# Retention and a mixture of experts in one kernel: moving work and tests at the seams between stages

## The chip, the cores and the metric

The kernel runs on one core of one Trainium2 chip. The metric is the device time of one execution in microseconds. A core has five engines that run side by side and wait for each other by semaphores: TensorE (PE in the profile; PEld is its loading of the stationary operand), VectorE (DVE), ScalarE (ACT), GpSimd (POOL) and SyncE (SP). Copies between memory and the core are started by an engine's queue and carried out by DMA engines.

## The reference, cut to what matters

Two blocks follow each other. The first is a retention layer: for each of 4 batches and 8 heads a 64x64 state decays and takes up one outer product per time step, over 768 steps. Its output, 3072 rows (tokens) of 512, goes to a mixture of experts: each token goes to the one expert out of 8 with the largest logit, whose two layers are 512 to 1024 and 1024 to 512.

```
state = gamma * state + k[t] v[t]^T          # per batch and head
y[t]  = q[t] @ state / sqrt(64)
x = y, heads side by side: (3072, 512)
logits = x @ w_gate;  e = argmax(logits);  gate = softmax(logits)[e]
out = gate * (max(x @ w1[e], 0) @ w2[e])     # no token is dropped, however many an expert gets
```

## The kernel before

The retention is computed in 24 steps of 128 time steps, ordered so that the four batches of one chunk make a group; there are 6 groups. A step loads q, k and v (`load`), scales and transposes them (`scale_and_transpose`), and does the masked products and the state (`retain`).

After each group, `place` finds each of its 512 tokens' expert, gate and rank within the expert, and stores the gated rows x to memory. It is written as a generator: each `yield` ends a piece, and the main loop takes a few pieces after each step, so that they lie between the matmuls of later steps.

```python
def place(c):                       # cut
    ... parts = wg^T x  (4 matmuls of 512 columns), lgT = copy          # L314, L317
    yield
    ... lg (logits), max, exp, one-hot oh, gate                         # L321 to L340
    yield
    rk = ... ; rank, col, prow, at, val, here                           # L343 to L373
    yield
    found = sum over b of here[b]^T val[b];  inv += found               # L377, L380
    yield
    x = xg[c % 2]
    for b in range(B):
        tr = ps("tr", 3, "trx")...
        for dt in range(DT):
            nc.tensor.transpose(tr[:, dt, :], xT[:, dt, b, :], ident)   # L388
        nc.scalar.activation(out=x[:, b, :]..., in_=tr, func=AF.Copy, scale=gate[:, b : b + 1])
        if b == 1:
            yield
    nc.scalar.dma_start(x_d[ts(c, B * P), :]..., x)                     # L393
    if c == NC - 2:
        ... tot, pad: at least 256 tokens of expert 0
        early.append(index(inv[:, :, 0 : EARLY // P], "_e"))
        gather(xs2[0], early[0][0], range(EARLY // P), (c + 1) * B * P)  # L160
```

The main loop and the **fixed job**: the first 256 tokens of expert 0 are known after five groups, so their two layers are computed while the sixth group is placed.

```python
for n in range(len(steps)):
    if n + AHEAD < len(steps): load(n + AHEAD)
    if n == 17: wa = weights(first, 0)
    if n + 1 < len(steps): scale_and_transpose(n + 1)
    retain(n)
    for _ in range(2 if n < len(steps) - B else 3): next(rest, None)
    if steps[n][1] == B - 1: rest = place(steps[n][0])

with tc.manual_schedule(engines={PE}):
    turn(xs2[0], xTa, range(EARLY // P), nc.vector.tensor_copy)     # transposes of gathered rows, L190
    for f in range(FT):
        layer1(EARLY, xTa, wa[0], hTa, f)                           # L198, ScalarE relu L200
        if f != 4: next(rest, None)
    for _ in rest: pass
    for t in range(EARLY // P):
        layer2(EARLY, hTa, wa[1], oa, t)                            # L210, ScalarE copy L213
scatter(oa, early[0][1], range(EARLY // P))                         # L217
```

Then the tokens per expert are counted, and for each expert an **arm** is chosen: the same job compiled for a number of rows, in steps of 32 up to 512. Engines load the arm's number into a register and branch. `switch_hint` tells an engine ahead of time where it will branch to.

```python
cnt = ...; nc.tensor.matmul(cnt, lhsT=ones_b, rhs=acc[:, NC, :], ...)   # L446
ne, arm = ...                        # VectorE, L449 to L457
src_i, dst_i = index(inv, "")        # rows to gather and to scatter, for all experts
...
sets = [wa, weights(keep2, 1)]       # keep2 takes memory that the fixed job's tiles held
with tc.manual_schedule(engines={PE, ACT, POOL}):
    gather(xs2[1], cols[0][0], range(HALF, TC))      # the rest of expert 0
    gather(xs2[0], cols[1][0], range(TC))            # expert 1
    which = regs(0)                                  # value_load of arm, L481
    tc.switch_hint(which, arms_of(0), label="job0")
    xT = mp.tile(...)
    turn(xs2[1], xT, range(HALF, TC), nc.vector.tensor_copy)
    for e in range(E):
        nxt = regs(e + 1)                            # not for the last
        for a in tc.Switch(which, arms_of(e), hint=f"job{e}"):
            n = STEP * (LEAST + a)
            ... 8 x layer1; turn of the next expert's rows; layer2 per 128 rows; the last job scatters in its arm
        scatter(...); gather(... e + 2); weights(... e + 2)

more = nc.values_load(over[0:1, 0:1], min_val=0, max_val=1)             # L520, on every engine
with tc.If(more > 0), ...:                                              # L521
    ... further jobs for experts with more than 512 tokens; with the given inputs not taken
```

Of the kernel before, what the change touches and what calls it, by code (L numbers as in the profile page):

```python
# [54 lines left out]
def kernel(  # L55
# [47 lines left out]
    nc.sync.dma_start(dec, decay)  # L103
# [119 lines left out]


    with ExitStack() as actx:
# [80 lines left out]
        def place(c):  # L306
# [34 lines left out]
            yield  # L341
            rk = ps("tr", 3, "rk")[:, 0 : B * E].rearrange("p (b e) -> p b e", e=E)
# [38 lines left out]

            yield

            x = xg[c % 2]
            for b in range(B):
                tr = ps("tr", 3, "trx").rearrange("p (a t) -> p a t", a=DT)
                for dt in range(DT):
                    nc.tensor.transpose(tr[:, dt, :], xT[:, dt, b, :], ident)  # L388
                nc.scalar.activation(out=x[:, b, :].rearrange("p (a t) -> p a t", a=DT), in_=tr, func=AF.Copy,
                                     scale=gate[:, b : b + 1])  # L390
                if b == 1:
                    yield
            nc.scalar.dma_start(x_d[ts(c, B * P), :].rearrange("(b p) r -> p b r", p=P), x)  # L393
            if c == NC - 2:

# [7 lines left out]
                early.append(index(inv[:, :, 0 : EARLY // P], "_e"))  # L403
                gather(xs2[0], early[0][0], range(EARLY // P), (c + 1) * B * P)
# [9 lines left out]
        xTa = keep.tile([P, DT, EARLY], F32, tag="xTa", name="xTa")  # L414
# [3 lines left out]
        for n in range(len(steps)):  # L418
            if n + AHEAD < len(steps):
                load(n + AHEAD)  # L420
            if n == 17:
                wa = weights(first, 0)
            if n + 1 < len(steps):
                scale_and_transpose(n + 1)
            retain(n)
            for _ in range(2 if n < len(steps) - B else 3):
                next(rest, None)
            if steps[n][1] == B - 1:
                rest = place(steps[n][0])


        with tc.manual_schedule(engines={mybir.EngineType.PE}):
            turn(xs2[0], xTa, range(EARLY // P), nc.vector.tensor_copy)
            for f in range(FT):
                layer1(EARLY, xTa, wa[0], hTa, f)
                if f != 4:
                    next(rest, None)
            for _ in rest:
                pass
            for t in range(EARLY // P):  # L440
                layer2(EARLY, hTa, wa[1], oa, t)
        scatter(oa, early[0][1], range(EARLY // P))


    cnt = ps("lg", 1, "cnt")[:, 0:E]
    nc.tensor.matmul(cnt, lhsT=ones_b, rhs=acc[:, NC, :], start=True, stop=True)  # L446
    ne = rt([P, E], "ne")
    arm = rt([P, E], "arm", I32)
    nc.vector.tensor_copy(ne, cnt)  # L449

    STEP, LEAST, MOST = 32, P // 32, W // 32
    nc.vector.tensor_scalar(out=arm, in0=ne, scalar1=float(STEP - 1), scalar2=None, op0=ALU.add)
    nc.vector.tensor_single_scalar(arm, arm, STEP.bit_length() - 1, op=ALU.arith_shift_right)
    nc.vector.tensor_scalar(out=arm, in0=arm, scalar1=float(LEAST), scalar2=float(MOST), op0=ALU.max, op1=ALU.min)
    nc.vector.tensor_scalar(out=arm, in0=arm, scalar1=-float(LEAST), scalar2=None, op0=ALU.add)

    nc.vector.tensor_scalar(out=arm[:, 0:1], in0=arm[:, 0:1], scalar1=-float(EARLY // STEP), scalar2=0.0, op0=ALU.add,  # L457
                            op1=ALU.max)
    src_i, dst_i = index(inv, "")
    PE, ACT, POOL = mybir.EngineType.PE, mybir.EngineType.Activation, mybir.EngineType.Pool  # L460
# [4 lines left out]
    o2 = [keep2.tile([P, TC, DM], F32, tag=f"o{i}", name=f"o{i}") for i in range(2)]  # L465
    for t in o2:
        nc.vector.memset(t, 0.0)
    sets = [wa, weights(keep2, 1)]
    cols = [(src_i[:, ts(e, TC)], dst_i[:, ts(e, TC)]) for e in range(E)]
    HALF = EARLY // P  # L470
    most = rt([P, 1], "most")
    over = rt([P, 1], "over", I32)
    nc.vector.tensor_reduce(most, ne, axis=AX.X, op=ALU.max)
    nc.vector.tensor_scalar(out=over, in0=most, scalar1=float(W), scalar2=None, op0=ALU.is_gt)

    def arms_of(e):
        return MOST - LEAST + 1 - (EARLY // STEP if e == 0 else 0)

    def regs(e):
        engines = [PE, ACT] + ([POOL] if e == E - 1 else [])  # L480
        return {g: nc.engines[g].value_load(arm[0:1, e : e + 1], min_val=0, max_val=arms_of(e) - 1) for g in engines}  # L481

    with tc.manual_schedule(engines={PE, ACT, POOL}):

        gather(xs2[1], cols[0][0], range(HALF, TC))
        gather(xs2[0], cols[1][0], range(TC))
        which = regs(0)
        tc.switch_hint(which, arms_of(0), label="job0")
        xT = mp.tile([P, DT, W], F32, tag="xTs", name="xTs")
        turn(xs2[1], xT, range(HALF, TC), nc.vector.tensor_copy)  # L490
        for e in range(E):
            w1t, w2t = sets[e]
            skip = EARLY if e == 0 else 0
            last = e == E - 1
# [4 lines left out]
            for a in tc.Switch(which, arms_of(e), hint=f"job{e}"):  # L499
                n = STEP * (LEAST + a)  # L500
                for f in range(FT):
                    layer1(n, xT[:, :, skip:], w1t, hT, f)
                if not last:
                    turn(xs2[e % 2], xTn, range(TC), nc.scalar.copy)
                tiles = -(-n // P)
                for t in [tiles - 1] + list(range(tiles - 1)):
                    if not last and t == max(tiles - 2, 0):
                        tc.switch_hint({g: nxt[g] for g in (PE, ACT)}, arms_of(e + 1), label=f"job{e + 1}")
                    layer2(n, hT, w2t, o2[e % 2], t)
                    if last:  # L510
                        scatter(o2[e % 2], cols[e][1], [t])
# [6 lines left out]


    more = nc.values_load(over[0:1, 0:1], min_val=0, max_val=1)  # L520
    with tc.If(more > 0), tc.tile_pool(name="op", bufs=1) as op:  # L521

        def ot(shape, name, dt=F32):
            return op.tile(shape, dt, tag=name, name=name)


        jobs_i, jobs, jend, jbeg = ot([P, E], "jobs_i", I32), ot([P, E], "jobs"), ot([P, E], "jend"), ot([P, E], "jbeg")
        nc.vector.tensor_scalar(out=jobs_i, in0=ne, scalar1=float(W - 1), scalar2=float(W), op0=ALU.add, op1=ALU.max)
        nc.vector.tensor_single_scalar(jobs_i, jobs_i, W.bit_length() - 1, op=ALU.arith_shift_right)
        nc.vector.tensor_scalar(out=jobs, in0=jobs_i, scalar1=-1.0, scalar2=None, op0=ALU.add)  # L530
        ones_e = ot([P, E], "ones_e")
# [42 lines left out]
        for j in range(OV):  # L574
# [6 lines left out]
            for f in range(FT):  # L581
                layer1(W, xT, w1t, hT, f)
# [28 lines left out]
```

## Time and profile before

Three runs took 554.88, 554.93 and 557.82 us; the median is 554.93. The profiled execution spans 553.5 us, with a mean granted TensorE clock of 0.983.

| stretch of the profiled run, us | what runs there | TensorE busy, us |
|---|---|---|
| 0 to 12 | first loads and transposes | 6.5 |
| 12 to 155 | retention, 24 steps, and placing | 138.9 |
| 155 to 184 | first layer of the fixed job, placing of the sixth group | 24.4 |
| 184 to 202 | second layer of the fixed job, count, registers | 14.8 |
| 202 to 541 | the eight jobs | 337.3 |
| 541 to 553.5 | last scatter and the program's end | 0 |

In the tables by stretch, a row gives the stretch, its length, and then busy time and number of instructions of PE, PEld, DVE, ACT and POOL, the granted clock, the DMA share and GB/s. In the lists by time, a row gives the start, the busy time, the engine, the line, what is written and read, and in brackets how long the engine had been idle and what it is thought to have waited for. An `x8` counts the profile's records; a float matmul leaves two.

### The profile page before, as it was taken

The page shows a single profiled execution, that of the slowest core. Times are in us where ns is not written, and L with a number is a line of the kernel's source. Part 1 is how long each engine was busy: PE and PEld are TensorE (multiplying, and loading weights), DVE is VectorE, ACT ScalarE, POOL GpSimd, SP SyncE. Part 2 cuts the span into 40 slices and gives each one's busy share as a digit, 9 for nine tenths or more (in the row PEclk, how much of TensorE's full clock was granted, in tenths as well). Part 3 has the DMA queues.
Part 4 walks back from the last instruction along what each step waited for, and adds up shares of the span by engine and source line. Part 5 has one row for each costly group of instructions (what it writes and reads, how often), then busy time and mean ns, then how long its engine had stood idle before and what let it go on. Part 6 is the DMA issues. An engine that isn't in the chain of part 4 may idle for free.

```text
span 553.5 us, 7883 instructions
## 1 busy us (share of the span) xinstructions
PE 521.9 (94%) x3228; PEld 320.9 (58%) x3228; DVE 87.9 (16%) x249; ACT 113.7 (21%) x227; POOL 101.3 (18%) x118
## 2 busy tenths in 40 slices
PE   6999999999969979999999999999999999999990
PEld 4778877877747565564555455456455545545540
DVE  2554546363613040000000000000000000000000
ACT  1223231423302112130121022013012102202100
POOL 7312221221010320300500230050050023011010
PEclk9999999999979989999999999999999999999996
DMA  9997877894210359512614251263261425000010
GB/s 184 203 212 187 189 194 153 213 341 116 75 39 1 120 210 333 211 48 107 212 61 154 73 191 45 110 211 104 117 209 51 154 69 208 1 23 36 4 41 23
DMA packets 96469, 72.45 MB, mean 131 GB/s; under 512 B 77946, under 2 KB 77946, under 8 KB 96384
## 3 DMA queue, kind: packets, MB, share of 16 engines
q1 hardware_dynamic: 88096, 52.48, 34.9%
q0 software_dynamic: 5120, 12.60, 6.1%
q10 hardware_dynamic: 3168, 6.29, 3.2%
q8 instruction: 47, 0.77, 0.6%
q14 instruction: 38, 0.31, 0.2%
HBM read 60.86 MB, written 14.68 MB: 136 GB/s over the span
## 4 chain that ended last, share of the span: by engine, by line
issue 51%; PE 33%; DMA 6%; POOL 4%; DVE 3%; SPq 0%; POOLq 0%; ACT 0%; DVEq 0%; ACTq 0%
PE y L300 5%; PE sc L273 5%; PE tr L249 5%; DMA out_dram<-o,dst 4%; PE hp L198 4%; PE ye L210 4%; PE y L296 3%; POOL xs L160 3%; PE new L283 2%; PE trx L388 2%; POOL out_dram L217 1%; PE parts L314 1%; PE lg L321 1%; DMA q<-in_q_dram 1%; PE trs L190 1%
## 5 line engine op out<-in xcount | busy, mean ns | idle before, releaser
L210 PE MATMUL ye<-w2t,hT 128*128 128x512 f32 (+3 forms) x640 | 164.1, 455 | 0.0
L198 PE MATMUL hp<-xTs,w1t 128*128 128x416 f32 (+4 forms) x512 | 162.7, 479 | 0.7 <-DMA w1t<-in_moe_w_dram 0.5
L198 PEld LDWEIGHTS hp<-xTs,w1t 128*128 128x128 f32 x512 | 93.0, 192 | 70.9 <-issue 55.7
L210 PEld LDWEIGHTS ye<-w2t,hT 128*128 128x128 f32 (+3 forms) x640 | 74.8, 154 | 84.4 <-issue 83.4
L217 POOL DMA_INDIRECT out_dram<-o,dst x30 | 29.9, 996 | 281.4 <-ACT o L213 275.6
L200 ACT ACTIVATE hT<-hp 128x416 f32<-128x416 f32 (+4 forms) x64 | 29.3, 481 | 136.9 <-PE hp L198 107.7
L213 ACT COPY o<-ye 128x512 f32<-128x512 f32 (+3 forms) x40 | 17.7, 444 | 144.8 <-PE ye L210 144.5
L256 POOL TENSOR_TENSOR vs<-v,dec 128x512 f32<-128x512 f32 x24 | 25.0, 1043 | 77.9 <-PE y L300 52.6
L160 POOL DMA_INDIRECT xs<-x_d,src x30 | 30.4, 1012 | 39.3 <-DMA x_d<-xg 30.5
L275 DVE TENSOR_TENSOR am<-sc,causal 128x512 f32<-128x512 f32 x48 | 31.4, 686 | 22.1 <-PE sc L273 22.0
L273 PE MATMUL sc<-qT,kT 64*128 64x128 f32 x384 | 33.6, 289 | 0.0
L300 PE MATMUL y<-am,vs 128*64 128x128 f32 x384 | 31.2, 280 | 1.0 <-DVE am L275 0.9
L273 PEld LDWEIGHTS sc<-qT,kT 64*128 64x128 f32 x384 | 26.7, 188 | 6.0 <-issue 4.7
L302 ACT COPY xTg<-y 128x512 f32<-128x512 f32 x24 | 14.1, 587 | 63.1 <-PE y L300 63.1
L300 PEld LDWEIGHTS y<-am,vs 128*64 128x64 f32 x384 | 22.7, 136 | 7.1 <-issue 4.1
L260 ACT COPY kT<-tr 128x512 f32<-128x512 f32 x24 | 14.1, 586 | 42.1 <-PE tr L249 42.0
L296 PE MATMUL y<-qT,state 64*64 64x128 f32 x320 | 22.7, 276 | 0.0
L259 DVE TENSOR_TENSOR qT<-tr,gqT 128x512 f32<-128x512 f32 x24 | 16.6, 691 | 37.5 <-PE tr L249 36.6
L190 PE MATMUL trs<-ident,xs 128*128 128x128 f32 x128 | 17.0, 287 | 5.8 <-issue 3.0
L190 PEld LDWEIGHTS trs<-ident,xs 128*128 128x128 f32 x128 | 15.0, 146 | 9.2 <-issue 5.3
L249 PE MATMUL tr<-ident,q 128*128 128x128 f32 x96 | 17.0, 299 | 2.2 <-DMA q<-in_q_dram 2.2
L296 PEld LDWEIGHTS y<-qT,state 64*64 64x64 f32 x320 | 17.3, 132 | 2.2 <-issue 0.3
(117 smaller groups left out, 275.4 us busy)
## 6 DMA issues: line engine op xcount, KB each, us to landing
w1t<-in_moe_w_dram SPq DMA_DIRECT2D x8, 2048.0 KB, 8.0
w2t<-in_moe_w_dram SPq DMA_DIRECT2D x8, 2048.0 KB, 11.8
q<-in_q_dram SPq DMA_DIRECT2D x24, 256.0 KB, 5.1
k<-in_k_dram SPq DMA_DIRECT2D x24, 256.0 KB, 4.9
v<-in_v_dram SPq DMA_DIRECT2D x24, 256.0 KB, 5.0
x_d<-xg ACTq DMA_DIRECT2D x6, 1024.0 KB, 5.1
xs<-x_d,src POOLq DMA_INDIRECT x30, 5.1
out_dram<-o,dst POOLq DMA_INDIRECT x30, 7.1
```

Source lines behind the costliest of these rows:

```text
L160: nc.gpsimd.indirect_dma_start(out=xs[:, t, :], out_offset=None, in_=x_d[0:rows, :], in_offset=bass.IndirectOffsetOnAxis(ap=idx[:, t : t + ...
L190: nc.tensor.transpose(tr[:, dt, :], xs[:, t, ts(dt, P)], ident)
L198: nc.tensor.matmul(hp, lhsT=w1t[:, 0, dt, ts(f, P)], rhs=xT[:, dt, 0:n], start=(dt == 0), stop=(dt == DT - 1))
L200: nc.scalar.activation(out=hT[:, f, 0:n], in_=hp, func=AF.Relu)
L210: nc.tensor.matmul(y[j * m : j * m + m, 0:c], lhsT=hT[:, f, t * P : t * P + m], rhs=w2t[:, 0, f, ts(j, c)], start=(f == 0), stop=(f == FT ...
L217: done = nc.gpsimd.indirect_dma_start(out=out[:, :], out_offset=bass.IndirectOffsetOnAxis(ap=idx[:, t : t + 1], axis=0), in_=o[:, t, :], i ...
L249: nc.tensor.transpose(tr[:, a, :], src[:, 2 * a : 2 * a + 2, :].rearrange("p h d -> p (h d)"), ident)
L256: nc.gpsimd.tensor_tensor(out=vs, in0=vt, in1=inner(dec[:, (1 + c) * H : (2 + c) * H], D), op=ALU.mult)
L273: nc.tensor.matmul(sc[j][:, a, :], lhsT=kT[r, a, :], rhs=qT[r, a, :], start=True, stop=True)
L275: nc.vector.tensor_tensor(out=am[j], in0=sc[j], in1=middle(causal[:, :], HP), op=ALU.mult)
L296: nc.tensor.matmul(y[r, a, :], lhsT=old[r, a, :], rhs=qT[r, a, :], start=(a == 0), stop=False, skip_group_check=True)
L300: nc.tensor.matmul(y[ts(j, D), a, :], lhsT=vs[:, 2 * a + j, :], rhs=am[j][:, a, :], start=(c == 0), stop=True, skip_group_check=True)
```

## The change

It moves work at four places.

- **x ahead of the ranks.** In `place` the transposes and the store of x stand right after the gate, ahead of ranks and index. The last steps of the loop take 4 pieces each. The gather for the fixed job is issued as soon as its index is there. The aim is that x is in memory earlier.
- **Count and next rows inside the fixed job.** The count, the arm numbers, the index, the gathers of the next rows, their transposes, the register loads and the first branch's hint stand between the first and the second layer's tiles. The second half of expert 0 goes to the same tile `xTa`, which moves to a pool that lives on.
- **Further jobs as a body of the last branch.** The test `over` and its `If` are gone. The last switch has one more arm, taken when any expert has more than 512 tokens, and all five engines branch there.
- **First retention ahead of second loads.** Step 0 is retained before step 1 is transposed, and the load of the decay table goes to ScalarE's queue.

```diff
-    nc.sync.dma_start(dec, decay)
+    nc.scalar.dma_start(dec, decay)
...
+    def arms_of(e):
+        return MOST - LEAST + 1 - (EARLY // STEP if e == 0 else 0) + (1 if e + 1 == E else 0)
+    def regs(e):
+        engines = [PE, ACT] + ([POOL, mybir.EngineType.DVE, mybir.EngineType.SP] if e + 1 == E else [])
...
+    def count():        # the lines that stood behind the fixed job, and:
+        nc.vector.tensor_reduce(most, ne, axis=AX.X, op=ALU.max)
+        nc.vector.tensor_scalar(out=over, in0=most, scalar1=float(W), scalar2=float(arms_of(E - 1) - 1), op0=ALU.is_gt,
+                                op1=ALU.mult)
+        nc.vector.tensor_tensor(out=arm[:, E - 1 : E], in0=arm[:, E - 1 : E], in1=over, op=ALU.max)
...                      # in place(): the block "x = xg[c % 2] ... dma_start(x_d ...)" moves up
             nc.vector.reciprocal(gate, gate)
+            yield
+            x = xg[c % 2]
+            ... transposes, scaled copies, a yield at b == 1
+            nc.scalar.dma_start(x_d[ts(c, B * P), :].rearrange("(b p) r -> p b r", p=P), x)
             yield
             rk = ...
...
             if c == NC - 2:
+                early.append(index(inv[:, :, 0 : EARLY // P], "_e"))
+                gather(xs2[0], early[0][0], range(EARLY // P), (c + 1) * B * P)
                 ... tot, pad
-                early.append(...); gather(...)
...
-        xTa = keep.tile([P, DT, EARLY], F32, tag="xTa", name="xTa")
+        xTa = first.tile([P, DT, EARLY], F32, tag="xTa", name="xTa")
...
+            if n == 0:
+                retain(n)
             if n + 1 < len(steps):
                 scale_and_transpose(n + 1)
-            retain(n)
-            for _ in range(2 if n < len(steps) - B else 3):
+            if n:
+                retain(n)
+            for _ in range(2 if n < len(steps) - B else 4):
                 next(rest, None)
...
             for f in range(FT):
                 layer1(EARLY, xTa, wa[0], hTa, f)
-                if f != 4:
+                if f not in (2, 5):
                     next(rest, None)
-            for t in range(EARLY // P):
-                layer2(EARLY, hTa, wa[1], oa, t)
+            arm, ne = count()
+            src_i, dst_i = index(inv, "")
+            gather(xs2[1], cols[0][0][:, HALF:], range(TC - HALF))
+            gather(xs2[0], cols[1][0], range(TC))
+            layer2(EARLY, hTa, wa[1], oa, 0)
+            turn(xs2[1], xTa, range(TC - HALF), nc.vector.tensor_copy)
+            which = regs(0)
+            tc.switch_hint(which, arms_of(0), label="job0")
+            layer2(EARLY, hTa, wa[1], oa, 1)
...
             for a in tc.Switch(which, arms_of(e), hint=f"job{e}"):
+                job(e, min(STEP * (LEAST + a), W), xT, xTn, hT, nxt)
+                if last and a == arms_of(e) - 1:
+                    further_jobs()
...
-    more = nc.values_load(over[0:1, 0:1], min_val=0, max_val=1)
-    with tc.If(more > 0), tc.tile_pool(name="op", bufs=1) as op:
```

## The prediction

> **What bounds the kernel now.** I read the page first (engine shares, the 40 slices, the costliest groups), then TensorE's instructions in order of time around each place where one stage hands over to the next. The page says that TensorE is the bound: 521.9 of 553.5 us, with 9s in nearly every slice.
>
> ```profile
> span 553.5 us, 7883 instructions
> PE 521.9 (94%) x3228; PEld 320.9 (58%) x3228; DVE 87.9 (16%) x249; ACT 113.7 (21%) x227; POOL 101.3 (18%) x118
> PE   6999999999969979999999999999999999999990
> PEclk9999999999979989999999999999999999999996
> ```
>
> So work of other engines is worth nothing by itself. What can be won is TensorE's idle time, 31.6 us, and matmuls at a low clock. Counted from 0, slices 11 and 14 (152 to 166 and 194 to 208 us), the first slice and the last are the only ones with less than 9, and the clock dips in the same two. A table by stretch puts the idle time in the same places; its first column after the stretch is its length, the next TensorE's busy time, and PEclk stands near the end of each line.
>
> ```profile
> 5.00:12.00 7.00, 5.39 (x32) 3.80 (x32) 1.38 (x2) 1.17 (x2) 5.34 (x6) 1.00 1.29 218
> 155.00:184.00 29.00, 24.38 (x130) 18.68 (x129) 6.33 (x31) 7.01 (x15) 1.62 (x2) 0.88 0.09 29
> 198.00:202.00 4.00, 1.93 (x9) 1.59 (x10) 1.23 (x4) 0.00 (x0) 0.81 (x1) 0.76 0.18 69
> 271.00:318.00 47.00, 47.00 (x193) 24.61 (x192) 0.00 (x0) 8.68 (x19) 8.06 (x9) 1.00 0.37 127
> 541.00:553.50 12.50, 0.00 (x0) 0.00 (x0) 0.00 (x0) 0.00 (x0) 0.72 (x1) 0.65 0.07 24
> ```
>
> A job in the middle (271 to 318) has no idle time, so only seams are left. The two large ones, in order of time:
>
> ```profile
> 147.95 0.37 ACTq L393 DMA_DIRECT2D x_d<-xg  x1
> 154.38 1.24 POOL L160 DMA_INDIRECT xs<-x_d,src_e  x1 [17.08 <-DVE am L275]
> 157.98 0.66 PE L190 MATMUL trs<-ident,xs 128*128 128x128 f32 x4 [2.03 <-DMA xs<-x_d,src_e]
> 159.48 1.11 PE L190 MATMUL trs<-ident,xs 128*128 128x128 f32 x4 [0.84 <-DMA xs<-x_d,src_e]
> 161.38 3.78 PE L198 MATMUL hp<-xTa,w1t 128*128 128x256 f32 x8 [0.78 <-DVE xTa L191]
> 166.50 1.99 PE L198 MATMUL hp<-xTa,w1t 128*128 128x256 f32 x8
> ...
> 196.73 0.17 PE L446 MATMUL cnt<-acc,ones_b 128*128 128x8 bf16 x1
> 199.86 1.72 PE L190 MATMUL trs<-ident,xs 128*128 128x128 f32 x8 [2.96 <-issue]
> 219.31 22.59 PE L198 MATMUL hp<-xTs,w1t 128*128 128x416 f32 x64 [0.47 <-DMA w1t<-in_moe_w_dram]
> ```
>
> First seam: x of the fifth group is stored at 147.95, gathered from 154.38, and TensorE waits 2.03 + 0.84 + 0.78 us before the fixed job's first layer, whose eight rows then take 3.78 us where the next eight take 1.99. The wait "DVE am" of the gather is misnamed: its index was written at 145.57, so it waited for the store (5.6 us to landing). Second seam: the count is taken after the whole fixed job, then the arm is worked out and loaded into registers while TensorE stands for 2.96 us.
>
> **What the Trainium skill says.** "TensorE: Matmul & The Clock Gate", Part 1, What's actually happening: after an idle window of about 3.4 us the array runs at half rate until it has been busy for about as long. The trace agrees: 3.78 against 1.99 us for the same eight rows, after a stretch from 155.95 to 159.4 with 0.66 us of work. "DMA: Bandwidth & Descriptors", Anatomy of one DMA, gives a fixed cost near 2 us plus bytes over 436 GB/s; for the 1 MB of x that makes an estimate of 4.4 us, and the trace has 5.1 to 5.6, which I use. "Perfetto Trace Analysis", Summary, says TensorE's reported end is an estimate; so I subtract starts, not add durations.
>
> **The change part by part.** No matmul is removed, so each part is worth what it takes from a seam. I follow TensorE's order in the new program.
>
> (a) Start. The decay load leaves SyncE's queue, so each load behind it starts 0.45 us earlier (issues at 0.82 and 1.27). The first retention no longer stands behind the second step's transposes, which waited 1.38 us for their q; but it needs v scaled by GpSimd (now at 8.57), so it fills only part of that hole. v comes 0.45 earlier, and I take **-0.6**.
>
> (b) The gather for the fixed job. For the fifth group the order is now: four heads of parts, transposes of x, logits, then the rest of a step, ranks, one-hot product. Parts end at 136.5 (137.03 less 0.6), ten transposes take 1.25, logits 1.0: 138.7. The gate came 1.7 us after the logits in the group before (113.0 to 114.7); I take 1.5 because a ScalarE copy no longer stands in between: 140.2. Four evictions take 2.42 (145.50 to 147.92): the store is issued at 142.6, not 147.95. With the same 6.43 from issue to gather: 149.0. The first tile landed 3.60 and the second 3.56 after its gather's start, 1.54 apart: 152.6 and 154.1. TensorE comes there at about 152.3 to 153.5. I count 13.7 us of work from 136.5, and three waits: 0.6 for an eviction before the fourth transpose, 1.2 for the ranks' one-hot rows (2.2 us on VectorE against 1.0 of filler), and 0.2 for the mask; the rest is an allowance for switches between short groups. The last retention's y is now put between the two transposed tiles. Then up to 0.8 for the second tile and 0.8 for its copy: the first layer starts near 157.0, not 161.38. That is -4.4, of which 0.6 is (a): **-3.8**.
>
> (c) Clock. With idle pieces under 1.2 us TensorE should stay at full speed. From the first layer's start to the second it took 5.12 (161.38 to 166.50); at full speed 1.75 for the rows (174.26 to 177.79 held two) and 1.0 for parts: **-2.4**.
>
> (d) The fixed job from its second row block to its end took 30.2 (166.50 to 196.73), plus 0.17 for the count. Transposes of x move from f 6 and 7 to f 3 and 4, ranks from f 2 to f 6, at no cost. Added: the transposes of the first job's second half, 0.94 at full clock (half of the 1.88 from 209.83 to 211.71 in a job), between the two tiles of the second layer. The one-hot product waits about 0.65 instead of 0.36, having one block of 1.74 to hide 2.4. **+1.0**. The gathers fit: x stored near 171, landed near 176; index ready near 177.3; tiles landed near 181 and 182.5; TensorE asks for them near 183.
>
> (e) From the end of the fixed job to the second job's first matmul: 22.4 before (196.90 to 219.31). Now the branch follows at once, with its hint one tile (6.9 us) ahead: 0.1, first layer at warm rate 7.16 (8 x 0.895, the spacing of its later evictions), transposes 1.88, second layer 7.13, 0.47 as before: 16.7. **-5.7**. This holds if the second job's weights are there. Their load waits for the last scatter of the fixed job: before, 3.9 us after TensorE was done (200.78), and it landed 9.1 to 10.5 later; so 14.4 at the latest against 16.7. That is close, and 0.4 us is set aside for it.
>
> (f) The end. The last scatter is issued at 540.74. Then GpSimd jumped out of the arm (to 543.3), loaded a flag (0.31), branched (543.7 to 545.4), added to its DMA semaphores (1.47), drained (547.4 to 552.7). Without the test one jump of 1.65 and the load go, but the semaphore step now stands inside the arm and waits for the landing near 543.4: 543.5 + 1.5 + 1.6 for the jump = 546.6 where the drain began at 547.4. **-0.8**.
>
> Sum: -0.6 - 3.8 - 2.4 + 1.0 - 5.7 - 0.8 + 0.4 = -11.9. From 554.93: **543.0 us**, 2.1% faster.
>
> **Rivals.** (1) The weights' load takes over as the second job's wait. For it: 2.3 us of slack, and the third set's load (2 MB, freed when the first job's first layer ends) now starts 3.5 us after the second set's instead of 9.2, on the same queue, which ran at 360 to 430 GB/s there. Against it: loads of one queue landed in order so far. It would give back 1 to 4 us: 544 to 547. (2) New stalls inside the last attention steps eat (b): the ranks now have one filler of 1.0 us, and the transposes of x are ahead of their gate. If TensorE reaches the gather 2 to 3 us later, the store's gain is worth little: 545 to 546, and if those holes add up to a cold array, (c) goes too: 548. (3) The first two seams are one: if the clock stays full through both, and hidden waits between short matmul groups (y took 1.47 at 115.92 where 1.09 is usual) go with them, more is won: 540 to 541. (4) The end is set by the drain of 5.3 us counted from the last DMA and not from the branch; then (f) is 0 or a little more than thought, within 1 us.
>
> **Range and chances.** The parts that rest on idle time which the page shows (seam one's 3.65, seam two's 2.96 and the cold rows) are about 10 of the 12 us, and rivals 1 and 2 each can take 2 to 4 of them. So 8 in 10: **540.0 to 547.0**. The line of 2% lies at 543.8, hardly above my number; rival 3 is as likely as rival 1. Faster by over 2%: 0.60; within 2%: 0.39; slower by over 2%: 0.01, as nothing was added to TensorE but order.
>
> **What would show it.** Right: the store of the fifth group's x issued near 142 to 143 and the fixed job's first layer at 156 to 158 with 1.8 to 2.0 us for eight rows; the fixed job ends near 191; no idle time over 0.5 us between it and the first job; the second job starts near 208; the clock is full in both seams; the last second-layer matmul ends near 529, and 13 us follow. Wrong: a wait for a weight load at the second job's start, over 3 us idle between 136 and 157, a 3.7 us block again, or the second to the eighth job together longer than the 320.6 us from 219.31 to 539.9.

## The result and the profile after

The changed kernel took 539.02 us (median of four, 538.93 to 539.41); the kernel before, run beside it, 556.38 (554.88 to 558.57). The ratio is 0.9686, with a 95% interval of 0.9645 to 0.9728: 3.1% faster, and 1 us below the predicted range. The profiled executions span 537.2 and 553.5 us, 16.3 apart, and this difference is taken apart below.

The page of the kernel after, its head and the 40 slices of TensorE:

```profile
span 537.2 us, 7881 instructions
PE 513.5 (96%) x3228; PEld 316.0 (59%) x3228; DVE 88.6 (16%) x250; ACT 113.8 (21%) x227; POOL 101.3 (19%) x118
PE   5999999999999999999999999999999999999991
PEclk9999999999999999999999999999999999999996
```

The two dips in the middle are gone from both rows. TensorE has the same 3228 instructions, but 8.4 us less busy time: those are matmuls that no longer run at half rate, and scores that come in fewer pieces (both below). Idle time fell by 7.9 us, from 31.6 to 23.7 (537.2 less 513.5). The table by stretch, for the places that answer to those of before:

```profile
5.00:12.00 7.00, 6.28 (x52) 5.35 (x52) 3.21 (x6) 0.59 (x1) 5.42 (x6) 1.00 1.36 218
149.00:178.00 29.00, 27.26 (x172) 20.75 (x172) 8.16 (x42) 7.59 (x16) 1.72 (x2) 1.00 0.15 53
186.50:190.50 4.00, 4.00 (x18) 2.33 (x17) 0.00 (x0) 0.59 (x1) 0.00 (x0) 1.00 0.01 4
257.00:304.00 47.00, 47.00 (x193) 24.56 (x193) 0.00 (x0) 8.69 (x19) 8.27 (x9) 1.00 0.37 128
527.00:537.20 10.20, 0.00 (x0) 0.00 (x0) 0.00 (x0) 0.00 (x0) 0.82 (x1) 0.56 0.08 28
```

From 5 to 12 us TensorE did 52 matmul records where it did 32; the stretch around the first seam is busy for 27.3 us of 29 instead of 24.4; the second seam is full; a job in the middle is as it was; the end takes 10.2 us instead of 12.5. In order of time:

```profile
140.36 0.37 ACTq L384 DMA_DIRECT2D x_d<-xg  x1
146.39 1.24 POOL L160 DMA_INDIRECT xs<-x_d,src_e  x1 [11.84 <-DVE pad L434]
155.38 1.99 PE L198 MATMUL hp<-xTa,w1t 128*128 128x256 f32 x8 [0.78 <-DVE xTa L191]
158.30 1.99 PE L198 MATMUL hp<-xTa,w1t 128*128 128x256 f32 x8
...
181.71 1.04 PE L190 MATMUL trs<-ident,xs 128*128 128x128 f32 x8
182.58 7.03 PE L210 MATMUL ye<-w2t,hTa 128*128 128x512 f32 x16
189.45 7.31 PE L198 MATMUL hp<-xTa,w1t 128*128 128x128 f32 x64
...
205.75 0.94 PE L198 MATMUL hp<-xTs,w1t 128*128 128x416 f32 x2
```

The store of x lands 4.3 us after its issue, near 144.7, and the first gather starts at 146.39, right behind its index:

```profile
145.94 0.15 DVE L175 SCALAR_TENSOR_TENSOR src_e<-tok_e,none_e 128x2 uint32<-128x2 f32 x1
```

In the kernel before it was the store that the gather waited for; now the index is written last. The transposes wait for no DMA now, the first eight rows take 1.99 us at once, and from 182.58 on nothing has a bracket: the first job follows the fixed job (7.31 us for its first layer), and the second job follows the first without a wait for its weights.

Checkpoints of the two profiled executions, in us, with the working of the last column: the difference of this row less that of the row before.

| checkpoint on TensorE | before | after | difference | of this piece | predicted |
|---|---|---|---|---|---|
| first group's parts | 34.98 | 31.81 | -3.17 | -3.17 | (a) -0.6 |
| fifth group's parts | 134.05 | 131.31 | -2.74 | +0.43 | 0 |
| first layer of the fixed job | 161.38 | 155.38 | -6.00 | -3.26 | (b) -3.8 |
| its second row block | 166.50 | 158.30 | -8.20 | -2.20 | (c) -2.4 |
| end of the fixed job | 196.90 | 189.45 | -7.45 | +0.75 | (d) +1.0 |
| second job's first matmul | 219.31 | 205.75 | -13.56 | -6.11 | (e) -5.7 |
| issue of the last scatter | 540.74 | 526.85 | -13.89 | -0.33 | 0, and +0.4 set aside |
| end | 553.5 | 537.2 | -16.3 | -2.4 | (f) -0.8 |

Two rows hold nearly all of the miss: the start and the end.

### The profile page after: what moved, and what is told of

The parts are those of the page before. It is cut to its first block, busy times and chain, and to the rows that moved or that the text cites. A ratio compares the mean times of both kernels' runs of the same rounds, so it can differ in the third digit from the quotient of the medians.

```text
span 537.2 us, 7881 instructions
## 1 busy us (share of the span) xinstructions
PE 513.5 (96%) x3228; PEld 316.0 (59%) x3228; DVE 88.6 (16%) x250; ACT 113.8 (21%) x227; POOL 101.3 (19%) x118
## 5 line engine op out<-in xcount | busy, mean ns | idle before, releaser
L198 PE MATMUL hp<-xTs,w1t 128*128 128x416 f32 (+3 forms) x448 | 154.2, 505 | 0.1
L198 PEld LDWEIGHTS hp<-xTs,w1t 128*128 128x128 f32 x448 | 85.0, 190 | 69.6 <-issue 54.5
L305 PE MATMUL sc<-qT,kT 64*128 64x128 f32 x384 | 31.5, 287 | 0.0
L305 PEld LDWEIGHTS sc<-qT,kT 64*128 64x128 f32 x384 | 25.5, 187 | 4.6 <-issue 4.4
L198 PE MATMUL hp<-xTa,w1t 128*128 128x256 f32 (+1 forms) x128 | 22.4, 330 | 1.4 <-DVE xTa L191 0.8
L291 DVE TENSOR_TENSOR qT<-tr,gqT 128x512 f32<-128x512 f32 x24 | 16.6, 691 | 31.6 <-PE tr L281 31.2
L198 PEld LDWEIGHTS hp<-xTa,w1t 128*128 128x128 f32 x128 | 19.0, 191 | 4.3 <-issue 1.3
```

Source lines behind the costliest of these rows:

```text
L198: nc.tensor.matmul(hp, lhsT=w1t[:, 0, dt, ts(f, P)], rhs=xT[:, dt, 0:n], start=(dt == 0), stop=(dt == DT - 1))
L305: nc.tensor.matmul(sc[j][:, a, :], lhsT=kT[r, a, :], rhs=qT[r, a, :], start=True, stop=True)
```

## Experiments

Kernels named "before + ..." hold one part of the change alone; those named "after ..." undo or alter one part. Each has its time beside runs of the kernel before on the same chip. "Parts" is the start of the first group's parts, "tail" the time from the issue of the last scatter to the end.

### The end: which wait does the drain stand behind?

**Before + further jobs as a body of the last branch** (s_tail):

```diff
-    more = nc.values_load(over[0:1, 0:1], min_val=0, max_val=1)
-    with tc.If(more > 0), ...:        # further jobs
+            if last and a == arms_of(e) - 1:
+                further_jobs()        # inside the arm; all five engines branch there
```

> The kernel before with only the further jobs as a body of the last branch. Theory fixed drain (the end is one jump and a drain of 5.3 us of its own length, and the semaphore step no longer stands behind the last scatter but beside it): 2.2 to 2.6 us less, 10.3 us from the last scatter's issue to the end instead of 12.8. Rival, the step of the prediction (the semaphore step waits for the last landing): 0.8 us less, 12.0 us from the last scatter's issue.

554.67 us, ratio 0.9975 (0.9956 to 0.9993): 1.4 us less, with an interval of 0.4 to 2.4. In the profiled execution the tail went from 12.76 to 10.52 us, 2.2 less. Its span is only 0.4 us shorter than that of before, because its start happened to be 1.6 us later (parts at 36.58 against 34.98; why comes with the start).

**After, with the test and its If back behind the switch** (a_notail), the same edit the other way round:

> The changed kernel with the test and its branch back behind the last job. Theory fixed drain: 2.2 to 2.6 us more than the changed kernel's 539.0, 12.8 us from the last scatter's issue to the end. Rival, the prediction's step: 0.8 us more.

541.90 us, ratio 0.9738 (0.9704 to 0.9772); tail 12.74 against 10.35. So the test costs 2.2 us in the tail of one surrounding and 2.4 in that of the other. GpSimd's own queue shows why. First the kernel before, where a row of a line's instructions gives the operation, its count, the shortest, median and longest time in ns, and the first and last start:

```profile
L520 POOLq TENSOR_LOAD <-over x1: 312/312/312, 543.3 to 543.3; - x1
L521 POOLq COMPARE_BRANCH  x1: 62/62/62, 543.7 to 543.7; - x1
L521 POOLq INC_SWDGE_SEM  x1: 1471/1471/1471, 545.9 to 545.9; - x1
L607 POOLq DRAIN  x3: 50/113/5299, 547.4 to 553.2; - x3
```

And the kernel after:

```profile
L586 POOLq INC_SWDGE_SEM  x1: 1453/1453/1453, 526.9 to 526.9; - x1
L617 POOLq COMPARE_BRANCH  x9: 33/33/70, 190.3 to 528.4; - x9
L617 POOLq DRAIN  x3: 46/113/5382, 531.0 to 536.9; - x3
```

The semaphore step (`INC_SWDGE_SEM`, 1.45 us, which adds to the semaphores of GpSimd's own DMA queue) starts at 526.9, beside the last scatter's own 0.98 us (526.85), and waits for nothing to land. Before, it started at 545.9, behind the jump, the load and the branch. In the kernel after, a jump follows (528.4), and the drain starts at 531.0: 4.15 us after the scatter's issue, where it was 6.66 (540.74 to 547.4). The drain takes 5.3 to 5.4 us whenever it starts.

### The two seams: apart and together

**Before + x ahead of the ranks** (s_x): the block of transposes, scaled copies and the store moves up, the gather ahead of `tot`, and the last steps take four pieces.

```diff
             nc.vector.reciprocal(gate, gate)
+            yield
+            ... transposes of x, scaled copies, dma_start(x_d ...)
             yield
             rk = ...
```

> The kernel before with only x stored ahead of the ranks (and 4 pieces a step at the end). Theory of the prediction, steps b and c: 5 to 6.5 us less than before, first layer of the fixed job about 3 to 4 us sooner after the fifth group's parts than before (27.3 us there), and its first eight rows in 1.8 to 2.0 us. Rival, the clock stays low there because the idle pieces before it (a wait for the transposes' eviction, one for the one-hot rows, one for the copy) add up to a cold window: 3 to 4 us less, eight rows in over 3 us.

550.67 us, ratio 0.9896 (0.9862 to 0.9930). From the fifth group's parts to the first layer it took 24.1 us instead of 27.3, and the first rows ran at full rate. But the second seam was as it had been:

```profile
159.44 1.99 PE L198 MATMUL hp<-xTa,w1t 128*128 128x256 f32 x8 [0.78 <-DVE xTa L191]
192.61 0.17 PE L445 MATMUL cnt<-acc,ones_b 128*128 128x8 bf16 x1
195.73 1.94 PE L190 MATMUL trs<-ident,xs 128*128 128x128 f32 x8 [2.95 <-issue]
197.91 7.98 PE L198 MATMUL hp<-xTs,w1t 128*128 128x128 f32 x64 [0.23 <-DVE xTs L191]
```

**Before + count and next rows inside the fixed job** (s_count): the lines of the count, the index, the gathers, the transposes and the registers move between the two tiles of the second layer; x is stored where it was.

```diff
+            arm, ne = count();  src_i, dst_i = index(inv, "");  gather(...);  gather(...)
             layer2(EARLY, hTa, wa[1], oa, 0)
+            turn(xs2[1], xTa, ...);  which = regs(0);  tc.switch_hint(...)
             layer2(EARLY, hTa, wa[1], oa, 1)
```

> The kernel before with only the count, the gathers, the register load and the hint inside the fixed job; x of the sixth group is still stored at f 6 and 7. Theory linked seams (the next rows can only be gathered when x is stored, 5 us after 182.3, and land 3.5 us later, so that the transposes between the two tiles of the second layer now wait 1 to 3 us): 2 to 4 us less. Rival, independent parts (steps d and e of the prediction as they stand): 4.7 us less or more.

552.80 us, ratio 0.9928 (0.9902 to 0.9954). Its timeline:

```profile
162.51 3.78 PE L198 MATMUL hp<-xTa,w1t 128*128 128x256 f32 x8 [0.78 <-DVE xTa L191]
192.55 1.06 PE L190 MATMUL trs<-ident,xs 128*128 128x128 f32 x8 [0.62 <-DMA xs<-x_d,src]
194.30 7.12 PE L210 MATMUL ye<-w2t,hTa 128*128 128x512 f32 x16 [0.68 <-issue]
```

The 2.96 us between fixed job and first job are gone, but 0.62 + 0.68 us of new waiting stand inside the fixed job: x of the sixth group is stored at 184.12, so its rows come too late for the transposes that now want them.

**Before + both** (s_xcount):

> The kernel before with both: x ahead of the ranks, and the count inside the fixed job. Theory linked seams: 10 to 12 us less, more than the sum of the two alone by 1 to 3 us. Rival, independent parts: the sum of the two alone within 1 us.

545.41 us, ratio 0.9795 (0.9760 to 0.9830). The store of the sixth group's x is issued at 171.48, and the transposes have no wait:

```profile
185.26 1.04 PE L190 MATMUL trs<-ident,xs 128*128 128x128 f32 x8
193.00 7.31 PE L198 MATMUL hp<-xTa,w1t 128*128 128x128 f32 x64
```

From the fifth group's parts to the second job's first matmul: 85.26 us before, 79.33 with x alone (-5.9), 82.69 with the count alone (-2.6), 74.92 with both (-10.3). The sum of the two alone is -8.5, so 1.8 us come only when both are there. Not all of that is the link. Up to the second row block s_count took 0.65 us longer than before (33.10 against 32.45), with more rows at half rate in the first seam, where its edit has no part. From the second row block to the second job the four took 52.81, 52.33, 49.59 and 47.94 us: here both together give 4.87 and the sum of the two alone is 3.70. So the link is worth about 1.2 us, near the 0.62 + 0.68 of new waiting in s_count: the count inside the fixed job needs the early store.

### The start: three edits of two lines

**Before + step 0 retained first** (s_retain), **before + decay load on ScalarE's queue** (s_dec), **before + both** (s_start):

```diff
-    nc.sync.dma_start(dec, decay)
+    nc.scalar.dma_start(dec, decay)          # s_dec, s_start
...
+            if n == 0: retain(n)             # s_retain, s_start
             scale_and_transpose(n + 1)
-            retain(n)
+            if n: retain(n)
```

> The kernel before with only step 0 retained ahead of step 1's transposes; the decay load stays on SyncE's queue. Theory order (the first retention's matmuls fill the hole in front of step 1's loads and keep TensorE busy, so that its clock rises 2 to 2.5 us earlier): 1.5 to 3.2 us less than before, parts of the first group at 32 to 33.5 instead of 34.98. Theory loads (the first 35 us wait for the loads' queue, and the decay's move is what counts): under 0.7 us less. Theory both (only a late but unbroken start warms the array): under 1.5 us less.

> The kernel before with only the decay load moved to ScalarE's queue. Theory order: within 0.6 us of before. Theory loads: 2 to 3 us less. Theory both: under 1.5 us less, or more time than before, because the decay lands later (3.8 instead of 2.6 us) and the scaling copy beside the memsets takes 1.8 instead of 0.4 us.

> The kernel before with both edits of the start. All theories: about 3.2 us less, parts of the first group near 31.8, as in the changed kernel. If it is under 1.5 us less, the start's gain in the changed kernel came from elsewhere.

553.65 us, ratio 0.9954 (0.9937 to 0.9972); 553.67, 0.9962 (0.9945 to 0.9978); 552.26, 0.9944 (0.9913 to 0.9975). By the ratios that is 2.6, 2.1 and 3.1 us less, with intervals of over 1.8 us each, which do not tell them apart. In the profiled executions the parts start at 34.19, 33.52 and 31.51 against 34.98. The first of these is not typical: that execution took 555.80 us, 2.15 above the median of its 20. So how the two edits add up on the kernel before is not shown. Both together reach what the whole change reaches (31.81), so the start's gain has nothing to do with the seams.

**After, with the whole start undone** (a_nostart) and **after, with only the decay load back on SyncE's queue** (a_decsp):

> The kernel after, with its start undone: decay load on SyncE's queue, and step 1 transposed ahead of step 0's retention. If the start is worth what it was worth alone on the kernel before (about 3.2 us, the same as the profile's 34.98 to 31.81), the time is 541.5 to 543 with the first group's parts at 34.5 to 36.5 us. If the start is worth only the 0.6 us of the prediction, and the rest was the chance of when the clock rises, the time is 539.3 to 540.3.

> The kernel after, with only the decay load back on SyncE's queue; step 0 is still retained first. If the order of the first retention makes the gain (TensorE without a hole, so that the clock rises early), the time is within 1 us of the kernel after, 538.5 to 540, and TensorE's first transposes begin near 3.2 us instead of 5.7. If the earlier loads make it, 541 to 542.5.

542.76 us, ratio 0.9778 (0.9753 to 0.9803), parts at 35.10; and 540.81, 0.9738 (0.9710 to 0.9766), parts at 33.09. So the order of the first retention is worth 2.0 us (35.10 to 33.09) and the decay load's queue 1.3 (33.09 to 31.81). Neither is the 0.45 us of one issue. Two things stand behind these numbers: half rate at the start, and cut blocks. TensorE at the start of the kernel after:

```profile
5.72 1.09 PE L281 MATMUL tr<-ident,gq_all 128*128 128x128 f32 x4 [5.72 <-DVE gq_all L442]
6.60 1.06 PE L281 MATMUL tr<-ident,q 128*128 128x128 f32 x4
7.45 1.06 PE L281 MATMUL tr<-ident,k 128*128 128x128 f32 x4
8.45 1.11 PE L315 MATMUL new<-vs,k 128*64 128x64 f32 x14
9.49 1.16 PE L305 MATMUL sc<-qT,kT 64*128 64x128 f32 x16
```

And with the decay load on SyncE's queue (a_decsp):

```profile
3.13 1.09 PE L281 MATMUL tr<-ident,gq_all 128*128 128x128 f32 x4 [3.13 <-POOL sel L117]
...
8.39 1.12 PE L315 MATMUL new<-vs,k 128*64 128x64 f32 x14 [1.43 <-POOL vs L288]
9.44 2.08 PE L305 MATMUL sc<-qT,kT 64*128 64x128 f32 x16
11.45 0.47 PE L315 MATMUL new<-vs,k 128*64 128x64 f32 x2
11.86 0.93 PE L281 MATMUL tr<-ident,q 128*128 128x128 f32 x4
```

The kernel after starts 2.6 us later, because the decay table lands later and its copy takes 1.79 us beside a clear on GpSimd, where it took 0.43 before; but then it has no hole. Its scores take 1.16 us at 9.49, as they do later on: the full rate. The other's take 2.08: nearly half rate. (PEclk reads 1.00 in both; the half rate shows only in how long the same instructions take.) The moment of the full rate can be read from the block that straddles it: with its first h us at half rate, a block takes h/2 more than at full rate. In a_decsp this is the transposes at 11.86, with 0.93 us where 0.66 is usual, so h is 0.54 and the moment 12.4; in the kernel after it is 9.5, between two blocks. So a_decsp works 7.3 us at half rate (12.4 - 3.13, less 1.95 of holes) and the kernel after 3.8 (9.5 - 5.72): 1.75 us lost, less 0.65 of idle time saved, is 1.1 of the measured 1.3.

The other 2.0 us come from order. Here are the scores of two steps of the kernel before, which transposes step 1 ahead of step 0's retention:

```profile
24.10 0.48 PE L273 MATMUL sc<-qT,kT 64*128 64x128 f32 x2
...
26.12 1.16 PE L273 MATMUL sc<-qT,kT 64*128 64x128 f32 x14
...
28.21 0.71 PE L273 MATMUL sc<-qT,kT 64*128 64x128 f32 x4
...
30.45 0.71 PE L273 MATMUL sc<-qT,kT 64*128 64x128 f32 x4
```

And of the kernel after:

```profile
18.83 1.16 PE L305 MATMUL sc<-qT,kT 64*128 64x128 f32 x16
...
23.24 1.16 PE L305 MATMUL sc<-qT,kT 64*128 64x128 f32 x16
```

One step's scores are eight matmuls (16 records). In one block TensorE goes on after 1.09 us; with one matmul cut off it takes 0.41 + 1.08. Where blocks are cut is the scheduler's choice: it fills in transposes of the next step. The new order of the first two steps leaves fewer cuts in the steps that follow, up to the first group's parts. Busy time of the scores up to the parts, in the groups by line, for before, after, a_decsp and a_nostart in turn (busy us and mean ns behind the bar):

```profile
L273 PE MATMUL sc<-qT,kT 64*128 64x128 f32 x80 | 8.4, 295 | 0.0
```

```profile
L305 PE MATMUL sc<-qT,kT 64*128 64x128 f32 x80 | 6.3, 286 | 0.0
```

```profile
L305 PE MATMUL sc<-qT,kT 64*128 64x128 f32 x80 | 7.2, 317 | 0.0
```

```profile
L305 PE MATMUL sc<-qT,kT 64*128 64x128 f32 x80 | 8.8, 309 | 0.0
```

Less their half-rate shares (0.2, 0, 0.9, 0.6) that is 8.2, 6.3, 6.3 and 8.2: the same 80 records cost 1.9 us more in the old order, with or without the rest of the change. A busy time counts the overlap at the end of each piece, though. Counted from start to start, the four are 7.5, 5.85, 5.85 and 7.5: 1.65 us for four more cuts, about 0.4 each. That is most of the 2.0; a_nostart also worked 0.4 us longer at half rate and stood idle 0.15 us longer.

**After, with the loops of the score matmuls exchanged** (a_pair), to see what a cut takes away:

```diff
-            for a in range(HP):
-                for j in range(2):           # j: half of the partitions
+            for j in range(2):
+                for a in range(HP):
```

> The kernel after with the two loops of the score matmuls exchanged: all four of one half of the partitions first, then all four of the other, where they alternated. Alternating, eight take 1.16 us (spacing 1.09); blocks that the scheduler split took 0.48 for one, 0.71 for two. If neighbours on different halves of the partitions run side by side and a split takes that away, a block of eight now takes 1.9 to 2.1 us, in 24 steps 17 to 23 us more: 556 to 562. If a split costs only by the switch to another kind of matmul, the block stays at 1.1 to 1.3 us and the time at 538.5 to 541.

545.49 us, ratio 0.9851 (0.9813 to 0.9890). A block of eight takes 1.71 us where the kernel after has 1.16; further down a block with one matmul cut off:

```profile
62.86 1.71 PE L305 MATMUL sc<-qT,kT 64*128 64x128 f32 x16
...
69.76 0.49 PE L305 MATMUL sc<-qT,kT 64*128 64x128 f32 x2
...
70.76 1.49 PE L305 MATMUL sc<-qT,kT 64*128 64x128 f32 x14
```

So the alternating order is worth 0.55 us a block, less than the 0.8 expected. Of 24 x 0.55 = 13.2 us only 6.2 reach the fixed job's first layer (155.38 to 161.56): the scheduler made another order with fewer cuts (none up to the first group's parts), and waits elsewhere shrink, those ahead of the one-hot products for instance from 4.3 to 1.7 us. "TensorEngine Tiling (Array Packing)", Key Properties, in the Trainium skill says that tiles of the array work independently and that a change of tiling mode drains it. The 0.55 us agree with the first, but each half also writes a tile of its own, so the exchange changes that too, and no run parts the two. For the second there is a hint: without a neighbour on the other half to lose, a cut costs 0.20 us here (0.42 + 1.42 from start to start, against 1.64 for the whole block), where it costs 0.40 in the alternating order. So about half of a cut's cost goes with the lost neighbour, if these blocks are typical.

### Can the start be made shorter still?

**After, with GpSimd's two clears moved out of the start** (a_mem), and the same **with the decay load on SyncE's queue** (a_mem_sp). Each clear takes 1.8 us and stands ahead of the first v. They were put into the loop's eighth and tenth step; the scheduler placed them right behind the first v.

```diff
-    for t in xs2:
-        nc.gpsimd.memset(t, 0.0)
...
+            if n in (8, 10): nc.gpsimd.memset(xs2[n // 2 - 4], 0.0)
```

> The kernel after, with the two clears of the gathered-rows tiles by GpSimd (1.8 us each, at 3.5 and 5.6) moved from the start into the eighth and tenth step of the loop. If those clears hold the start (the copy of the first q takes 1.79 us beside one of them, and the first v waits for the other), the first group's parts start 1 to 2.5 us earlier than 31.8, and the time is 536.5 to 538. If the start is bound by the loads or by the clock instead, it is 538.5 to 539.5, the same as after.

> As the one before, with the decay load also back on SyncE's queue. If the clears hold the start and the queue of the decay load does not matter, 536.5 to 538, as with the clears moved alone. If the decay load's place matters by itself by the 0.45 us of one issue, 0.3 to 0.8 us slower than with the clears moved alone. If both clears and loads do not matter, 538.5 to 539.5.

541.16 us, ratio 0.9748 (0.9723 to 0.9774), and 541.75, 0.9763 (0.9738 to 0.9789); parts at 34.08 and 34.36. The first matmul came 1.3 us earlier (4.38), and yet the parts 2.3 later, which neither theory had. The copy of the decay table took 0.43 us again, but a hole of 0.78 us opened ahead of the first v, full rate came at 13.2, and the scores are cut again (8.4 us busy; 0.9 of it is half rate). An earlier start is no gain where it comes with holes and another order.

**After, with twelve matmuls of zeros ahead of the data** (a_warm), **a_mem with nine of them** (a_mem_warm), **after with six** (a_warm6). Nothing reads what they write.

```diff
+    fill = const.tile([P, 512], BF16, ...);  nc.vector.memset(fill, 0.0)
+    for _ in range(12): nc.tensor.matmul(ps("lg", 1, "warm"), lhsT=fill[:, 0:P], rhs=fill, start=True, stop=True)
```

> The kernel after, with twelve matmuls of zeros (128x512 bf16[...]) on TensorE before the first data, from about 0.8 to 5.7 us; nothing reads what they write. If the time at which the array reaches its full rate is what the start is worth, all real matmuls run at full rate from 5.7 on; the first v (ready at 8.4) then becomes the wait, so the first group's parts start at 31.0 to 31.4 instead of 31.8, and the time is 538.2 to 538.8. If the rate does not depend on work before, parts at 31.8 to 32.5.

> The kernel after with the two clears moved behind the first v, as before, and nine matmuls of zeros on TensorE before the first data (to about 4.4 us). The moved clears alone made the parts of the first group start at 34.1, with the full rate from about 13 us. If that late rise of the clock was their loss, parts start at 30.3 to 31.3 and the time is 537.5 to 538.5, the shortest of all. If the loss came from the other order of the instructions or from the clears beside the loop, parts start at 33.5 to 34.3 and the time is about 541.

542.74 us, ratio 0.9753 (0.9719 to 0.9788), and 542.87, 0.9753 (0.9717 to 0.9788); parts at 34.72 and 34.73. Both missed. One such matmul took about 0.62 us (1.27 to 8.72 for twelve), so they ran until 8.7 and 6.8 and not to 5.7 and 4.4, past the time when the data were there, and the scheduler, which counted them too, put the later instructions in another order (scores busy 9.2 us in a_mem_warm). That run had its full rate at about 8.0, the earliest of all, and was no faster: the cut scores (2.5 us against after, from start to start) and the late first data (1.1) ate it.

> The kernel after with six matmuls of zeros ahead of the data instead of twelve. In the run with twelve, one took 0.64 us[...], so that they ran until 8.7 and pushed the first data back by 3 us, and the scheduler put the score matmuls in another order. Six should end at 5.1, before the data (5.7), and the order of TensorE's later instructions is that of the kernel after, word for word. If the rise of the clock counts by itself, the full rate comes by about 8 us at the latest, the first group's parts start at 31.0 to 31.5 (31.81 in after) and the time is 538.0 to 538.8. If matmuls of zeros do not raise the clock, 31.7 to 32.0 and 538.8 to 539.5.

539.76 us, ratio 0.9728 (0.9703 to 0.9753). Here the order is that of the kernel after and the zeros end before the data:

```profile
1.28 3.81 PE L107 MATMUL warm<-fill 128*128 128x512 bf16 x6 [1.28 <-DVE fill L105]
5.71 1.09 PE L285 MATMUL tr<-ident,gq_all 128*128 128x128 f32 x4 [0.63 <-DVE gq_all L446]
...
9.48 1.94 PE L309 MATMUL sc<-qT,kT 64*128 64x128 f32 x16
```

The full rate came at about 11.0, later than without zeros. The profiled executions that have one order of TensorE's instructions up to the parts can be set side by side:

| start | executions | full rate at, us | parts at, us |
|---|---|---|---|
| of before | before, a_nostart, s_xcount, s_x, s_count, s_tail | 12.3, 12.8, 13.3, 14.8, 14.8, 16.2 | 34.98, 35.10, 35.27, 35.87, 35.93, 36.58 |
| of after | s_start, after, a_notail; with zeros a_warm6 | 8.5, 9.5, 10.1; 11.0 | 31.51, 31.81, 32.12; 32.58 |

A later full rate costs a little under half a microsecond per microsecond. "TensorE: Matmul & The Clock Gate", Part 1, What's actually happening, in the Trainium skill says that the window in which activity is counted runs freely, so the moment varies by about 500 ns from run to run; it does vary here, but by more, 3.9 us in the first row. So 1.6 us of the old start and 0.6 of the new one differ between executions with one and the same order. Yet the rows do not meet: the gain of the new start is no chance, and the profile of before happens to be the earliest of its row. Matmuls of zeros bought nothing that can be seen in this spread. None of these versions beat the kernel after.

## Why the prediction was wrong

**The bound and the seams: right.** TensorE's idle time and half-rate rows were what there was to win. (b), (c), (d) and (e) were each within 0.6 us, and their sum, -10.9 predicted, was -10.8 measured; that the errors (+0.54, +0.2, -0.25, -0.4) cancel so well is luck. The store came at 140.36 (142.6 predicted; 2.1 of that is the start), the first layer at 155.38 with 1.99 us, the second job at 205.75. In (b) one wait was another than thought: the gather started 6.03 us after the store's issue, near the 6.43 taken, but it was the index that it waited for, and the store had landed 1.7 us before. This cost nothing: at the 3.6 us that such a gather took before, its first rows were there near 150, and TensorE asked for them at 151.82. (The 4.4 us that the prediction works out for the store come from a section on copies that GpSimd issues; this one goes by ScalarE's queue and took 4.3 to 5.6. No term of the sum rests on it.) (e) was 0.4 better: the 0.47 us ahead of the second job, counted "as before", were gone.

**(a), the failing step: -0.6 predicted, -3.17 measured.** It said: "v comes 0.45 earlier, and I take -0.6". It priced the edit as holes filled and issues moved, and the holes hardly changed (5.7 us of idle time up to the parts, 5.5 before). What changed was how long the same instructions take: 1.65 us for cut scores, shown by the times from start to start, while the pair a_nostart and a_decsp, which differ in that order alone, lies 2.0 apart; and about 1.3 for a full rate that comes at 9.5 instead of 12.3 us (half of 6.8 less 3.8 us of work at half rate, less 0.2 of idle time more). 0.2 are left over. How large the second part comes out in one execution is in part chance; that the full rate comes earlier is not, as the table of executions shows. Half rate at the start could have been read from the profile of before: its first transposes took 1.09 to 1.12 us for four records where later ones take 0.66. The cut blocks stand there too; which cuts the new order would leave does not.

**(f), the second failing step: -0.8 predicted, -2.4 measured.** It said: "the semaphore step now stands inside the arm and waits for the landing near 543.4". It waits for no landing: it starts beside the scatter (526.9 and 526.85), 2.7 us sooner than taken, and the jump behind it took 2.6 us where 1.6 were taken; so the 6.66 us up to the drain shrank to 4.15, and not to 5.86. s_tail and a_notail show the same in both surroundings. Rival (4), a drain counted from the last DMA, is refuted: from the end of the last scatter's instruction to the drain's start it was 5.7 us before and is 3.2 now, and the drain is as long as it was.

**The rivals.** (1) did not happen: the second job's weights were loaded from 193.55, 12.2 us ahead of its first matmul, which did not wait for them; the 0.4 us set aside were not needed. (2) took 0.5 us at most: (b) was -3.26, not -3.8, and TensorE still waited 0.53, 0.75 and 0.78 us in the last attention steps. (3) was the right direction, and for its stated reason in part: the seams are linked (about 1.2 us, s_xcount), but this was inside the sum; the 540 to 541 it gave was passed because of (a) and (f), which it did not have in mind.

In terms of the sum, measured less predicted in the spans: (a) -2.6, the stretch to the fifth group +0.4, (b) +0.5, (c) +0.2, (d) -0.25, (e) -0.4, jobs and allowance -0.7, (f) -1.6: -4.4, from -11.9 to -16.3. The mechanism of the change was seen; the two smallest terms were mis-sized, and both in one direction.

What stays open: how much of the 1.3 us of the clock another pair of executions would show (each kernel has one profiled execution), and what the two halves of a cut's 0.40 us are.

## What to carry to other kernels

Price a change of order by the time of the blocks it cuts or joins, not only by the holes it fills: the 64-partition matmuls here cost 1.09 us for eight in one block and 1.49 with one cut off. At the start, an unbroken late beginning can beat an early one with holes. And at the program's end, ask of each step on the last queue what it waits for: what stands behind a branch can often stand beside the last DMA.

## What the runs showed of the hardware

- GpSimd's drain at the program's end took 5.30 to 5.38 us in before, after, s_tail and a_notail, wherever it started; its semaphore step for software DMA took 1.45 us beside a scatter and 1.47 alone.
- The same 128x512 copy on VectorE took 0.43 us alone (before, a_mem) and 1.79 us beside a GpSimd clear of 128x2048 (after: 3.79 to 5.58 us, the clear 3.50 to 5.29).
- A bf16 matmul of 128x512 at the start, one behind the other into one buffer, took about 0.62 us each (a_warm).
- PEclk reads 1.00 from 5 to 12 us in before and after, although TensorE's first blocks there take up to twice as long as the same blocks later.
